# Turned weight blocks 14 to 17 placed behind the next period's scores, two late q units one or two loops later, half of w_out one loop earlier

## The chip, the core and the metric

The kernel runs on one core of a Trainium2 chip. That core has five engines with queues of their own, each served strictly in order: TensorE (PE: matmuls and transposes, results in PSUM), VectorE (DVE), ScalarE (ACT), GpSimd (POOL) and SyncE (SP, which here issues DMA only). The metric is device time in microseconds for one execution; the time of a kernel is the median of its runs.

## The reference, cut to what matters

Attention over 8 batches of 8 heads, 576 tokens and head size 64, in which each row keeps only the scores within `tau` of its maximum, and behind it a two-layer network on the 4608 tokens.

```python
scores = scale * np.matmul(q, k.transpose(0, 1, 3, 2))
thresh = np.max(scores, axis=-1, keepdims=True) - tau
scores = np.where(scores >= thresh, scores, -1000000000.0)
attn = np.exp(scores - np.max(scores, axis=-1, keepdims=True))
attn = attn / (np.sum(attn, axis=-1, keepdims=True) + 1e-09)
out = np.matmul(attn, v)
...
h = x @ w_in                      # 4608x512 by 512x2048
g = np.maximum(0.01 * h, h)
return (g @ w_out).astype(np.float32)
```

## The kernel before, in words

The attention is cut into *periods*. A period is one batch `b`, one quarter `m` of its first 512 query tokens (or the 64-token tail, `m == 4`) and two of the four pairs of heads; it has four score tiles of 128 queries by 576 keys. The order of all instructions is written out by hand: one `while` loop (L633) issues, in its turn `n`, the scores of period `n` (`st`), the turning of the weights of period `n-1` (`before`) and the value product of period `n-2` (`due`, since `PV_LAG` is 2). Each engine executes its own instructions in the order in which the loop issued them. In the text, "loop 3" is turn `n == 3`.

In one loop turn the work goes like this:

- `scores(st)` (L302) multiplies q by k on TensorE into the PSUM tile `sc`, in three products of fp16 halves (high by high, low by high, high by low). A marker instruction on another queue (`SIGNAL`, L279, POOL's or SP's) orders two pieces that share a bank. VectorE reads each tile out, negates it and takes the minimum (`copy_min`, L336).
- The first `plain` tiles get their weights from an exponential on ScalarE (`exp_plain`, L364) and a masking product on VectorE (`weights`, L376). The others get them from two ScalarE passes, a steep one and an exponential (`exp_steep`, L369: a "steep pair", lines 372 and 373). `plain` is 2 for the first two periods and 3 from then on.
- A period's weights, 18 blocks of 128 by 64 in pairs, must be turned. From period 3 on a DMA transpose issued by SP does it (`turn_w`, L387). For periods 0 to 2 (`here`) TensorE does it (`turn_w_here`, L393) and the result is copied from PSUM (`take_w`, L401): blocks 0 to 5 by way of an `h` bank, 6 to 13 and 14 to 17 by way of the one `o` bank. Blocks 14 to 17 are turned at the end of loop `n`, after the copy of blocks 6 to 13 by ScalarE, and ahead of `scores` of loop `n+1` (L752 to L760).
- `pv(due)` (L418) multiplies the turned weights by v, `evacuate` (L432) scales by the reciprocal row sums (`spread` turns these on TensorE, ScalarE copies them to `by`), and two periods make one group of 128 tokens for the network. `layer1` (L456, into `hp`, then ScalarE's leaky step to `g`) and `layer2` (L473, into `o`) are handed out over the loop turns, up to two of the first and four of the second in each.
- PSUM holds `sc` in five banks, two banks with the tag `h` (turned q and k, `by`, `pv`, `hp`, late units) and one with the tag `o`.
- q and k reach TensorE turned and split into two fp16 halves. For batch 0 units of the raw fp32 data are turned on TensorE (`turn32`, L196), and ScalarE writes the high half (`take_high`, L228), VectorE the low half (`take_low`, L234). Which unit is due in which loop stands in the tables `early32` and `late32` (L575 to L580). The unit `q32[s, 2]` covers token blocks 2 and 3 of head pairs `2s` and `2s+1`; period 4 is the first to need `q32[0, 2]`, and period 5 the first to need `q32[1, 2]`. From batch 1 on POOL splits the data ahead of the turning (`split_pool`).
- Loads: SP issues k, q and v, and the weight transposes stand on the same queue. `load_w` (L121) loads w_in (0 to 3) and w_out (4 to 7) in eight DMAs of 512 KB issued from POOL's queue, with a cast to fp16; `pool_at` names the loop turn.
- `idle(k, bank)` (L520) issues `2k` matmuls on blank data, whose result is not used. Loops 0 to 3 have some after the scores, and loop 3 twelve more (24 matmuls) ahead of its first `layer1`.

Of the kernel before, what the change touches and what calls it, by code (L numbers as in the profile page):

```python
# [33 lines left out]
def kernel(  # L34
# [86 lines left out]
    def load_w(i):  # L121
        if i < 4:
            return nc.gpsimd.dma_start(out=w_in16[:, :, ts(i, 512)],
                                in_=moe_w_in[:, ts(i, 512)].rearrange("(a p) f -> p a f", p=128))
        else:
            j = i - 4
            return nc.gpsimd.dma_start(out=w_out16[:, ds(4 * j, 4), :],
                                in_=moe_w_out[ds(512 * j, 512), :].rearrange("(j p) f -> p j f", p=128))
# [378 lines left out]
    def at(d, n, f):  # L507
        d.setdefault(n, []).append(f)
# [17 lines left out]
    def spare(tag):  # L526
        return ps.tile([128, 512], FP32, tag=tag, bufs=2 if tag == "h" else 1, name="spare")
# [47 lines left out]
    early32[0] = [k32[2], [q32[1, 0]]]  # L575
    late32[0] = k32[3]
    early32[1] = [[q32[0, 1]]]
    late32[1] = [q32[0, 2]]
    early32[2] = [[q32[1, 1]]]
    late32[3] = [q32[1, 2]]  # L580
    def load_w_in():

        loads = [load_w(i) for i in range(4)]
# [6 lines left out]
        at(pool_at, 1 + p // 2, lambda p=p: cast_v(0, p))  # L590
    at(pool_at, 1, lambda: cast_vtails(0))
    for i in range(4):
        at(pool_at, 1 if i < 2 else 4, lambda i=i: load_w(4 + i))

    def split_at(n, key):
        at(split_at_, n - 1, key)
# [35 lines left out]
    n = 0  # L632
    while n < N + PV_LAG or l1q or pending or l2q or stores:  # L633
        st = periods[n] if n < N else None
        before = periods[n - 1] if 1 <= n <= N else None
        due = periods[n - PV_LAG] if PV_LAG <= n < N + PV_LAG else None
        here = before and before.n < 3
        plain = 2 if n < 2 else 3
        keys, now32, late = turns_at.get(n, []), early32.get(n, []), late32.get(n)


        if n == 0:
            def between():
                copy_min(st, 0)
                copy_min(st, 1)
                take_low(k32[1])
                for x in now32:
                    turn32(x)
            scores(st, between)
            turn32(late)  # L650
        elif st:
            scores(st)
        bank = turn(keys) if keys else None
        for x in now32 if n else []:
            turn32(x)
        if here:
            before.wt = sb.tile([128, 2, 9, 128], FP16, tag="wT", bufs=4, name="wT")
            bank = ps.tile([128, 1024], FP16, tag="h", bufs=2, name="tp")
        if due:
            bank = spread(due, bank)  # L660
        if here:
            turn_w_here(before, 0, 6, bank[:, 0:768])
        for key in keys:
            take(key, 0, on_act)
        if due:
            take_spread(due, bank)
        for x in now32:
            take_high(x)
        if here:
            take_w(before, 0, 6, bank[:, 0:768], on_act)  # L670
        if st:
            copies(st, before, lambda: [take(key, 1, on_dve) for key in keys], now32)
            exp_plain(st, 0)
            if n == 0:
                exp_plain(st, 1)
                take_high(late)
                take_low(late)
        elif before:
            recip(before)
        work = [lambda key=key: split_pool(key) for key in split_at_.get(n, [])] + pool_at.get(n, [])  # L680
        for i, f in enumerate(work):
            mm = f()
            if i == 0 and before:
                behind_masks(mm, before)
        for key in keys:
            if key[1:] == ("t", "k"):
                widen_keys(key[0])
        if n >= 5:

            for f in small_at.get(n, []):  # L690
                f(small=nc.gpsimd)
        if n < 4:
            idle((4, 10, 8, 4)[n], spare("o"))
        if here:
            o = ps.tile([128, 1024], FP16, tag="o", bufs=1, name="wp")
            if n < 3:
                turn_w_here(before, 6, 8, o)
        elif before and st:
            turn_w(before)
        for f in loads_at.get(n, []) + (small_at.get(n, []) if n < 5 else []):  # L700
            f()
        while stores and (n >= N or n not in loads_at or len(stores) > 1):
            store()

        if due and (n == 3 or n > N):
            pv(due)
            if n > N:
                evacuate(due)
        if n == 3:
            turn_w_here(before, 6, 8, o)  # L710
            idle(12, spare("h"))
        for half in range(2):
            if half == 1 and n == 3:
                exp_steep(st, 3)
            for _ in range(2):
                if l2q:
                    layer2()
            if l1q:
                layer1()
            elif n >= N:  # L720
                settle()
            if half == 0:
                if st:
                    for i in range(1, plain if n else 0):
                        exp_plain(st, i)
                if here:
                    take_w(before, 6, 8, o, on_act)
                if late and n not in (0, 3):
                    turn32(late)
                    take_high(late)  # L730
                if n == N:

                    before.wt = sb.tile([128, 2, 9, 128], FP16, tag="wT", bufs=4, name="wT")
                    free = [(sc[:, ts(i, 512)].bitcast(FP16), 8 * i, m) for i, m in enumerate((8, 8, 2))]
                    for o, first, m in free:
                        turn_w_here(before, first, m, o)
                if due and n <= N:
                    if n != 3:
                        pv(due)
                    evacuate(due)  # L740
                if n == N:
                    a, *more = [take_w(before, first, m, o[:, 0 : 128 * m], on_dve if first else on_act)
                                for o, first, m in free]
                    for x in more:
                        tc.declare_no_dep(x.ins, a.ins, reason="other banks")
            elif st and n != 3:
                for i in range(plain, 4):
                    exp_steep(st, i)
        if n == 3:
            turn32(late)  # L750
            take_high(late)
        if here:  # L752
            o = ps.tile([128, 512], FP16, tag="o", bufs=1, name="wp")
            turn_w_here(before, 14, 4, o)
        for i in range(plain if st else 0):
            weights(st, i)
            if late and n and i == (2 if n == 3 else 0):
                take_low(late)
            if here and i == 1:
                take_w(before, 14, 4, o, on_dve)  # L760
        n += 1
# [1 line left out]
_INS = ['q', 'k', 'v', 'tau', 'moe_w_in', 'moe_w_out']  # L763
# [31 lines left out]
```

## Time and profile before

| | |
|---|---|
| median of 3 runs | 487.35 us (487.16 to 488.01) |
| the profiled execution | 485.95 us |
| its span, first to last instruction | 484.2 us |
| mean granted TensorE clock over the span | 0.996 |

Times in views of the profile are microseconds from the start of the span. A row of the timeline or of the chain gives the start, the length, the engine, the line of the kernel and the operation, as output `<-` inputs. Square brackets give the idle time of the engine just before, and what ended it. Groups give busy time and mean nanoseconds of one instruction. The "chain" is the work that ended last, followed back from the last instruction. A chain row's length is the time for which it held the chain; the same instruction's row in the timeline has its own length.

### The profile page before, as it was taken

To read this page: it belongs to the slowest core of one execution; us is meant where nothing else is said; L and a number is where in the kernel's file an instruction comes from. 1 tells how busy PE (TensorE), PEld (TensorE's weight loads), DVE (VectorE), ACT (ScalarE), POOL (GpSimd) and SP (SyncE) were. 2 spreads that over 40 slices of the span, in tenths; PEclk is the share of its full clock that TensorE was granted. 3 is DMA by queue.
4 is the path that set the end of the run, shared out by engine and by line. 5 is a ranking of instruction groups with operands and counts; after the bars stand their busy time and mean duration, and the time that the engine had idled before them with its cause. 6 is when DMAs were issued, how large, how long until landed. Compare 5 with 4: busy or idle time off the path is not lost.

```text
span 484.2 us, 25192 instructions
## 1 busy us (share of the span) xinstructions
PE 465.3 (96%) x10834; PEld 377.4 (78%) x10834; DVE 433.1 (89%) x1311; ACT 420.5 (87%) x781; POOL 215.0 (44%) x353
## 2 busy tenths in 40 slices
PE   7878799999999999999999999999999999999996
PEld 5667688888888888888888778888878788777774
DVE  3988789999999999999999989999999999999940
ACT  4898588999999999999999989999999899988862
POOL 2636545554465464454465574454456473000000
PEclk9999899999999999999999999999999999999999
DMA  9999987799899989789899988979899997655541
GB/s 176 233 218 189 205 189 165 153 187 199 181 177 189 237 168 173 156 164 212 178 189 192 185 188 185 151 180 192 185 184 203 193 184 123 123 122 123 123 95 45
DMA packets 206752, 83.68 MB, mean 173 GB/s; under 512 B 175792, under 2 KB 201392, under 8 KB 206640
## 3 DMA queue, kind: packets, MB, share of 16 engines
q1 hardware_dynamic: 199728, 74.79, 80.1%
q0 software_dynamic: 5504, 6.82, 7.4%
q8 instruction: 85, 1.39, 1.2%
q10 hardware_dynamic: 1408, 0.46, 0.4%
q14 instruction: 27, 0.22, 0.2%
HBM read 36.70 MB, written 9.44 MB: 95 GB/s over the span
## 4 chain that ended last, share of the span: by engine, by line
PE 87%; ACT 6%; DMA 4%; DVE 1%; issue 1%; SPq 0%; POOL 0%; POOLq 0%; ACTq 0%
PE hp L466 25%; PE o L479 25%; PE sc L297 21%; PE pv L426 8%; DMA wT<-w 4%; PE tp L410 3%; PE tp L186 3%; ACT w L373 1%; ACT e L367 1%; ACT s L372 1%; ACT wT L402 1%; PE sc L523 1%; DVE s L338 1%; ACT g L469 1%; ACT qT L232 0%
## 5 line engine op out<-in xcount | busy, mean ns | idle before, releaser
L338 DVE TENSOR_SCALAR_CACHE_REDUCE s<-sc 128x576 f32<-128x576 f32 x288 | 205.3, 753 | 17.4 <-PE sc L297 17.1
L466 PEld LDWEIGHTS <-win 128*64 128x64 f16 x4608 | 147.1, 110 | 28.8 <-DVE xt L437 1.1
L378 DVE SCALAR_TENSOR_TENSOR w<-s,th,e 128x576 f16<-128x576 f32 x214 | 164.4, 815 | 0.6 <-DVE x L445 0.2
L367 ACT ACTIVATE e<-s,mn 128x576 f16<-128x576 f32 x214 | 158.3, 778 | 0.0
L479 PE MATMUL o<-wout,g 128*64 128x512 f16 x1152 | 149.4, 381 | 0.4 <-DMA wout<-in_moe_w_out_dram 0.4
L466 PE MATMUL hp<-x,win 128*64 128x128 f16 x4096 | 137.1, 220 | 0.4 <-DVE kT L249 0.4
L469 ACT ACTIVATE g<-hp 128x512 f16<-128x512 f32 x144 | 86.1, 598 | 44.0 <-PE hp L466 43.9
L297 PE MATMUL sc<-kT,qT 64*128 64x384 f16 (+7 forms) x1920 | 120.5, 284 | 2.4 <-SPq L331 0.9
L297 PEld LDWEIGHTS <-qT 64*128 64x128 f16 (+1 forms) x1920 | 89.8, 97 | 19.7 <-SPq L331 2.0
L160 POOL TENSOR_SCALAR scaled<-raw 128x512 f32<-128x512 f32 x53 | 32.7, 616 | 148.2 <-DVE w L378 128.1
L479 PEld LDWEIGHTS <-g 128*64 128x64 f16 x1152 | 58.6, 110 | 29.6 <-issue 0.7
L171 POOL TENSOR_TENSOR half<-scaled,half 128x512 f16<-128x512 f32 (+1 forms) x68 | 71.7, 1054 | 5.8
L373 ACT ACTIVATE w<-s,minus_tau 128x576 f16<-128x576 f32 x74 | 57.4, 776 | 2.4
L372 ACT ACTIVATE s<-s,th 128x576 f32<-128x576 f32 x74 | 56.8, 767 | 0.7 <-DVE th L356 0.7
L426 PE MATMUL pv<-wT,v 128*64 128x128 f16 (+1 forms) x1600 | 53.0, 214 | 4.0 <-DMA wT<-w 2.8
L426 PEld LDWEIGHTS <-v 128*64 128x64 f16 x1600 | 45.8, 110 | 4.9 <-issue 4.0
L167 POOL CAST half<-scaled 128x512 f16<-128x512 f32 (+1 forms) x68 | 38.2, 562 | 4.4
L445 DVE TENSOR_TENSOR x<-pv,by 128x256 f16<-128x256 f32 x64 | 27.1, 424 | 8.1 <-PE pv L426 6.5
L416 ACT COPY by<-tp 128x256 f16<-128x256 f16 x72 | 26.8, 372 | 1.1 <-PE tp L397 1.1
L186 PEld LDWEIGHTS <-half 64*128 64x128 f16 x968 | 24.4, 95 | 3.5 <-DVE qT L239 1.4
L186 PE MATMUL tp<-ident,half 64*128 64x64 f16 x968 | 24.5, 190 | 1.0 <-DVE qT L239 1.0
L113 POOL CAST v<-vraw 128x256 f16<-128x256 f32 x64 | 24.0, 408 | 0.0
(61 smaller groups left out, 335.4 us busy)
## 6 DMA issues: line engine op xcount, KB each, us to landing
vraw<-in_v_dram SPq DMA_DIRECT2D x16, 512.0 KB, 5.4
out_dram<-osb SPq DMA_DIRECT2D x31, 256.0 KB, 4.0
raw<-in_q_dram SPq DMA_DIRECT2D x13, 512.0 KB, 4.9
raw<-in_k_dram SPq DMA_DIRECT2D x13, 512.0 KB, 5.1
win<-in_moe_w_in_dram POOLq DMA_DIRECT2D x4, 512.0 KB, 9.6
wout<-in_moe_w_out_dram POOLq DMA_DIRECT2D x4, 512.0 KB, 12.5
raw<-in_q_dram SPq DMA_DIRECT2D x12, 128.0 KB, 3.8
raw<-in_k_dram SPq DMA_DIRECT2D x10, 128.0 KB, 4.2
```

Source lines behind the costliest of these rows:

```text
L171: nc.gpsimd.tensor_tensor(out=halves[key][:, 1, 0:n, :, :], in0=scaled.pop(key)[:, 0:n, :, :], in1=halves[key][:, 0, 0:n, :, :], op=AX.sub ...
L186: nc.tensor.transpose(tps[key][r][:, x, t, :], half[rows, x, t, :, :].rearrange("p h d -> p (h d)"), ident[rows, rows])
L297: yield nc.tensor.matmul(out=o, lhsT=lhs, rhs=turned[st.b, "k"][rows, kx, pair, ds(key0, n)], start=(i == 0), stop=(i == 2), skip_group_ch ...
L338: return nc.vector.tensor_scalar(out=st.s[TILES[n]][:, :], in0=sc[:, ds(PLACE[TILES[n]], 576)], scalar1=-1.0 / UNIT, scalar2=None, op0=AX. ...
L367: nc.scalar.activation(out=st.e[t][:, :], in_=st.s[t][:, :], func=AF.Exp, bias=st.mn[:, n : n + 1], scale=-1.0)
L372: nc.scalar.activation(out=z, in_=z, func=AF.Prelu, bias=st.th[:, n : n + 1], scale=-1.0, alpha=1e20)
L373: nc.scalar.activation(out=w_of(st, t), in_=z, func=AF.Exp, bias=minus_tau[:, :], scale=1.0, accum_out=st.sum[:, c, h : h + 1])
L378: st.last = nc.vector.scalar_tensor_tensor(out=w_of(st, t), in0=st.s[t][:, :], scalar=st.th[:, n : n + 1], in1=st.e[t][:, :], op0=AX.is_le ...
L426: nc.tensor.matmul(out=st.pv[ds(64 * h, 64), c, ts(u, n)], lhsT=v16[st.b % 2][:, pair, blk, :], rhs=st.wt[:, c, blk - (blk > 4), ts(u, n)] ...
L466: nc.tensor.matmul(out=hp[ds(64 * c, 64), jj, :], lhsT=w_in16[:, i, ds(128 * (4 * u + jj) + 64 * c, 64)], rhs=g.x[:, i, :], start=(i == 0) ...
L469: nc.scalar.activation(out=g.g[:, ds(4 * u, 4), :], in_=hp[:, :, :], func=AF.Prelu, bias=0.0, scale=1.0, alpha=0.01)
L479: nc.tensor.matmul(out=g.o[ds(64 * c, 64), :], lhsT=g.g[:, j, ds(64 * c, 64)], rhs=w_out16[:, j, :], start=(j == 0), stop=(j == 15), skip_ ...
```

## The change

```diff
     early32[1] = [[q32[0, 1]]]
-    late32[1] = [q32[0, 2]]
+    late32[3] = [q32[0, 2]]
     early32[2] = [[q32[1, 1]]]
-    late32[3] = [q32[1, 2]]
+    late32[4] = [q32[1, 2]]
...
     for i in range(4):
-        at(pool_at, 1 if i < 2 else 4, lambda i=i: load_w(4 + i))
+        at(pool_at, 1 if i < 2 else 3, lambda i=i: load_w(4 + i))
...
         here = before and before.n < 3
-        plain = 2 if n < 2 else 3
+        rest = due and due.n < 3
+        plain = 2 if n < 2 or n == 4 else 3
...
         elif st:
             scores(st)
+        if rest:
+            o = ps.tile([128, 512], FP16, tag="o", bufs=1, name="wp")
+            turn_w_here(due, 14, 4, o)
         bank = turn(keys) if keys else None
...
         if st:
-            copies(st, before, lambda: [take(key, 1, on_dve) for key in keys], now32)
+            def taken():
+                for key in keys:
+                    take(key, 1, on_dve)
+                if rest:
+                    take_w(due, 14, 4, o, on_dve)
+            copies(st, before, taken, now32)
...
         if n == 3:
+            turn32(late)
             turn_w_here(before, 6, 8, o)
-            idle(12, spare("h"))
...
                         exp_plain(st, i)
+                if n == 3:
+                    take_high(late)
                 if here:
                     take_w(before, 6, 8, o, on_act)
...
-        if n == 3:
-            turn32(late)
-            take_high(late)
-        if here:
-            o = ps.tile([128, 512], FP16, tag="o", bufs=1, name="wp")
-            turn_w_here(before, 14, 4, o)
+        if n == 4:
+            take_low(late)
         for i in range(plain if st else 0):
             weights(st, i)
-            if late and n and i == (2 if n == 3 else 0):
+            if late and (n == 3 and i == 1 or n > 4 and i == 0):
                 take_low(late)
-            if here and i == 1:
-                take_w(before, 14, 4, o, on_dve)
         n += 1
```

It has five parts.

1. Blocks 14 to 17 of periods 0, 1 and 2 are turned at the start of the next loop turn, behind its scores (loops 2, 3 and 4), and VectorE copies them between the first and the second tile that it reads from the new scores.
2. The unit `q32[0, 2]` moves from loop 1 to loop 3 and `q32[1, 2]` from loop 3 to loop 4. In loop 3 the unit is turned ahead of blocks 6 to 13, its high half is written ahead of ScalarE's copy of these blocks, and its low half after VectorE's second weights. In loop 4 the low half is written ahead of the weights.
3. In loop 4 `plain` is 2: the third tile of period 4 gets its weights from a steep pair on ScalarE, and VectorE's product for it goes.
4. The last two of the four w_out loads are issued in loop 3, behind the splitting of the first k unit of batch 1, and no longer in loop 4.
5. The 24 matmuls on blank data in loop 3 go.

## The prediction

> **What bounds the kernel now.** I read the page first, then the granted clock and the DMA rate over stretches, then the chain of waits from the start to 120 us.
>
> ```profile
> PE 465.3 (96%) x10834; PEld 377.4 (78%) x10834; DVE 433.1 (89%) x1311; ACT 420.5 (87%) x781; POOL 215.0 (44%) x353
> ...
> L367 ACT ACTIVATE e<-s,mn 128x576 f16<-128x576 f32 x214 | 158.3, 778 | 0.0
> ...
> L373 ACT ACTIVATE w<-s,minus_tau 128x576 f16<-128x576 f32 x74 | 57.4, 776 | 2.4
> L372 ACT ACTIVATE s<-s,th 128x576 f32<-128x576 f32 x74 | 56.8, 767 | 0.7 <-DVE th L356 0.7
> ```
>
> TensorE is busy for 465.3 of 484.2 us, so only some 19 us are open, and the diff touches periods 1 to 4 alone. Every later period does the same work in the same order, so the question is how much earlier the kernel falls into step. Columns of the next rows: stretch, length, busy time of PE, PEld, DVE, ACT, POOL, then granted clock, DMA share, GB/s.
>
> ```profile
> 28.00:36.00 8.00, 7.57 (x169) 6.72 (x170) 6.66 (x22) 6.86 (x12) 2.38 (x3) 1.00 1.22 212
> 36.00:44.00 8.00, 6.60 (x154) 5.53 (x152) 7.19 (x22) 6.15 (x12) 3.89 (x5) 1.00 0.94 158
> 44.00:52.00 8.00, 7.78 (x181) 6.44 (x178) 7.47 (x24) 6.92 (x15) 4.42 (x7) 1.00 1.27 245
> 54.20:56.60 2.40, 0.02 (x1) 0.00 (x1) 1.00 (x4) 1.94 (x4) 2.40 (x6) 1.00 0.63 134
> 57.20:60.70 3.50, 3.50 (x49) 2.61 (x45) 2.64 (x7) 0.00 (x0) 0.47 (x1) 0.52 1.24 210
> ```
>
> From 54.20 to 56.60 TensorE does almost nothing, and right behind that, from 57.20 to 60.70, its clock is granted at 0.52. The chain of waits (start, length, what) names the cause:
>
> ```profile
> 44.95 11.54 DMA wT<-w
> ...
> 56.63 0.75 PE pv L426 x20
> 57.38 1.65 PE o L479 x8
> 59.02 1.71 PE hp L466 x32
> ```
>
> The weights of period 4 are turned by a DMA transpose issued at 44.95, which lands at 56.49; period 6's value product `pv` has to wait for it. The earlier part of the chain is a hand-over between ScalarE (ACT) and TensorE:
>
> ```profile
> 20.62 0.50 ACT qT L232
> ...
> 31.03 0.37 ACT by L416
> ...
> 37.06 0.50 ACT qT L232
> ...
> 39.33 1.08 PE hp L466 x32
> 40.42 0.56 PE pv L426 x20
> 40.98 0.86 PE o L479 x8
> 41.84 0.89 PE hp L466 x32
> 42.73 1.57 PE sc L297 x16
> ```
>
> One row of the timeline belongs between the first two:
>
> ```profile
> 28.43 0.41 PE L397 MATMUL wp<-ident,w 128*64 128x128 f16 x8 [2.35 <-ACT wT L402]
> ```
>
> At 28.43 the last four blocks of period 2's weights (`wp`, blocks 14 to 17 of 18) are turned as soon as ACT has copied blocks 6 to 13 out of the one `o` bank, and only behind them come the scores of period 3 and what ACT needs to go on at 31.03.
>
> **The change part by part. First: the four blocks go behind the scores.** The same 8 transposes (0.41 us on the path at 28.43) and the same copy by VectorE (DVE) remain, one loop turn later. What goes is the order "ACT copy, `wp`, scores, ACT". Between 28.43 and 31.03 lie 2.60 us, in which ACT has one steep pair to do, 0.767 + 0.776 = 1.54 us by the groups. So ACT idles for about 1.06 us there, and that is what the edit can return; the scores of period 3 then start when DVE has read the previous ones. The `o` bank still has one buffer, so `wp` now waits for it behind the scores. Queued behind that wait are the transposes for `by`, the idle matmuls and `pv`, and they need ACT's same copy or the one just before it anyway, so I cost the moved wait at nothing; without that cover it would cost the 0.41.
>
> **Second: the two late q units.** The first, two head pairs by two token blocks, leaves loop 1 for loop 3, which takes ACT's 0.50 at 20.62 off the path. The second leaves loop 3 for loop 4. In loop 3 there is thus one unit before and one after; it only stands earlier there, ahead of the weight copy. Together with the 1.06 ACT should reach the end of period 3 at 37.56 - 0.50 - 1.06 = 36.0. Before, the key transposes of period 4 also waited for the low half of that unit on DVE, and `hp` started at 39.33, 1.77 behind ACT's copy. Now they wait only for ACT's last `g`. If the whole 1.77 stays, `hp` starts at 37.8; if DVE's part of it (a third to a half) falls away, at 37.0. That is a lead of 1.5 to 2.3 us.
>
> Loop 4 gets the second unit, and its price stands here:
>
> ```profile
> 34.56 0.66 PE L211 MATMUL tp<-ident,raw 128*128 128x128 f32 x4
> ...
> 44.83 0.57 ACT L249 COPY qT<-tp 128x512 f16<-128x512 f16 x1
> ...
> 47.22 0.75 PE L426 MATMUL pv<-wT,v 128*64 128x128 f16 x20
> ```
>
> Four fp32 transposes cost 0.66 us of TensorE, ahead of `pv`, and since they take one of two `h` banks, `pv` now waits for ACT to empty `hp`: 0 to 0.6, I take 0.3. The scores of period 5 then start at 42.73 - 1.9 + 0.66 + 0.3 = 41.8, or 41.1 at the good end.
>
> **Third: `plain` is 2 in loop 4.** The third tile goes from a plain exponential on ACT (0.778) and a mask on DVE to a steep pair on ACT (1.54). This pair stands behind the second `hp`, where ACT had 42.73 to 44.83, 2.1 us, to its next copy. From 41.1 to 41.8 it is now 2.1 + 1.54, so that copy comes at 44.7 to 45.4 instead of 44.83. The lead is mostly spent on ACT. After it come on ACT `by`, a first exponential and `g`, whose `hp` is ready sooner than before, and then `pv`, until now at 47.22; there I take 0.4 us of lead as left (**term 1**). Bounds: the plain sum of ACT's changes in period 4 if none of the head start arrives, 0.50 + 1.54 - 0.78 = 1.26 against the 0.50 saved in loop 1, a loss of about 0.8, I keep -0.9; and the whole lead of TensorE at the good end, 42.73 - 41.1 = +1.6. My 0.4 lies nearer to the ACT side because the row at 44.83 sets what follows.
>
> **Fourth: w_out's second half one loop earlier.** The queue of SyncE (SP), which issues the transposes, and the landing of the w_out loads:
>
> ```profile
> 36.84 2.94 SPq L389 DMA_TRANSPOSE wT<-w  x1
> 39.88 0.51 SPq L75 DMA_DIRECT2D raw<-in_k_dram  x1
> 40.49 0.55 SPq L99 DMA_DIRECT2D vraw<-in_v_dram  x1
> 41.14 2.20 SPq L106 DMA_DIRECT2D vrawt<-in_v_dram  x2
> 44.95 7.92 SPq L389 DMA_TRANSPOSE wT<-w  x1
> ```
> ```profile
> wout<-in_moe_w_out_dram POOLq DMA_DIRECT2D x2, 512.0 KB, 10.2
> ```
>
> The last row is for the two loads issued from GpSimd's (POOL's) queue in loop 4. Issuing one transpose takes SP 2.94 us, and 7.92 when loads are backed up ahead of it. The 11.54 us are thus 7.92 of issue and 3.62 behind it. Ahead of it stand 1.15 MB from SP and 1.05 MB of w_out on POOL's queue. The DMA engines moved 158 GB/s from 36 to 44 us and 245 from 44 to 52. They can hold (245 - 158) x 8 us = 0.70 MB more in the first stretch. If w_out is in flight there already, SP's own 1.15 MB, issued from 39 to 43 us, drain alone at 245 GB/s in 4.7 us, by about 47 to 48. The transpose issued at 44.7 to 45.4 then has its issue over at 47.7 to 48.5 and lands at 51.3 to 52.1. TensorE wanted it at 54.2 (the start of the idle stretch) less term 1, near 53.8, so the wait of 54.2 to 56.63 goes: 2.4 us (**term 2**, bounds 0 and 2.4). On POOL the two issues move past the splitting of period 4's second unit, which is only done earlier; and they move ahead of the marker that releases the second half of period 4's scores, which at POOL's 44% busy hides them.
>
> With the wait goes the slow clock: `o` and `hp` at 57.38 and 59.02 took 1.65 + 1.71, against 0.86 + 0.89 at 40.98 and 41.84, so 1.61 us (**term 3**, bounds 0 and 1.61). Late next would be period 5's transpose; it stands behind the same SP queue, which moves up by some 4 us with it.
>
> **The idle matmuls** (24 in loop 3) lay in TensorE's slack while ACT was the chain; I cost their loss at nothing, and what it would cost without that cover is the clock case below. Trainium skill, "TensorE: Matmul & The Clock Gate", Part 4: PE-mode transpose, says that transposes do not count as TensorE activity for the clock as other matmuls do. Loop 3 loses real matmuls and gains transposes, so the page speaks against this edit; by it the sum would be that of the clock case. No stretch of this trace is made of transposes alone for long enough to settle it.
>
> **Sum.** 0.4 + 2.4 + 1.6 = 4.4 us. The profiled execution took 485.95 (its span of 484.2 and 1.75 around it), so 481.55; the runs' median lies 1.4 higher at 487.35, so 482.95, rounded to **483.0**.
>
> **The rivals.**
> *ACT eats more than the lead* (term 1 at -0.9, terms 2 and 3 as above): a gain of 3.1, **484.2**. For it: the row at 44.83. Against it: ACT is busy for only 6.15 of 8 us from 36 to 44.
> *The clock falls in loop 3.* After the idle 2.4 us at 54.20 it fell to 0.52; in loop 3 there would be mostly transposes for some 4 us. One `hp` and one block of scores, 1.08 + 1.57 us, would double, and about 1 us of that lies in slack: 1.6 lost, **484.6**. Against it: ahead of 28.43 TensorE idles for 2.35 us, and the clock of the stretch behind it (28 to 36 us) reads 1.00.
> *The load's move does not do what it is for*: the first w_out half is still moving when the second is issued, the same bytes pass, and the transpose lands at 56.49 as now. Then the wait swallows the lead: **487.35**. For it: the DMA share of 0.94 from 36 to 44. Against it: only 158 GB/s there.
> *The jam moves to period 3's transpose* (the slower side). This one is issued near 36.1, now right among the w_out loads. If it too takes 7.92 us, SP is free at 44.0 rather than 39.8, its three loads (3.46 us) end at 47.5, and period 4's transpose starts there. With 7.92 once more it lands at 47.5 + 7.92 + 3.62 = 59.0, 2.5 later than now: **489.8**. It decides the sign from the point where that landing passes 56.49, that is when both issues together are stretched by over 7.4 us. For it: w_out shares the engines with whatever is issued beside it. Against it: w_out is then the only load ahead, on another queue, and SP's has room.
>
> **How the numbers follow.** Forecast 0.60, ACT 0.12, clock 0.08, no change 0.08, jam 0.12. Two runs that differ by under 0.2% (1 us) can't be told apart. Faster: 0.60 + 0.12 + 0.08 = 0.80; within 0.2%: 0.08; slower: 0.12. The low end is 487.35 - (1.6 + 2.4 + 1.6) = 481.75, less 0.25 for the spread of the runs, 481.5. The high end takes in both faster rivals and a wait that goes only in part, 487.0; left out are the last two rivals.
>
> **What would show it.** Right: no TensorE wait on `wT` near 54 us, a granted clock of 1.00 from 52 to 62, the issue of period 4's transpose near 3 us instead of 7.92, the scores of period 3 before 28, `pv` of loop 5 at 46.5 to 47.4, and a steady state that begins 4 to 5 us earlier. The step on ACT is wrong if `pv` of loop 5 comes after 47.5 or before 46; the step on the loads if a transpose is issued for over 5 us between 35 and 50; and the prediction as a whole if `pv` still waits for `wT` in loop 5 or 6.

## The result and the profile after

| | before | changed |
|---|---|---|
| median of the runs | 487.16 us (486.45 to 488.01, 7 runs) | 484.70 us (482.95 to 486.71, 7 runs) |
| ratio, 95% interval | | 0.9949 [0.9925, 0.9972] |
| profiled execution, its span | 485.95, 484.2 us | 483.62, 481.9 us |
| mean granted clock of that execution | 0.996 | 1.000 |

Of all the runs in this document one, the 489.31 us among e9's four, is in a slower state, and the median and ratio of e9 below are of the other three.

The changed kernel is 2.5 us faster, inside the range that was forecast and 1.7 us above the forecast of 483.0. But the wait that the forecast made its gain from is still there. First the parts of TensorE's timeline of the changed kernel that mark its path: the scores (`sc`) of periods 3, 5, 7 and 9, the first `hp` of loop 4, and `pv` of loops 5, 6 and 7.

```profile
26.03 1.64 PE L297 MATMUL sc<-kT,qT 64*128 64x384 f16 x24
...
37.22 1.08 PE L466 MATMUL hp<-x,win 128*64 128x128 f16 x32 [0.29 <-DVE kT L249]
...
41.49 1.65 PE L297 MATMUL sc<-kT,qT 64*128 64x384 f16 x24
...
47.39 0.75 PE L426 MATMUL pv<-wT,v 128*64 128x128 f16 x20 [0.61 <-DMA wT<-w]
...
56.15 0.75 PE L426 MATMUL pv<-wT,v 128*64 128x128 f16 x20 [2.31 <-DMA wT<-w]
...
58.59 1.64 PE L297 MATMUL sc<-kT,qT 64*128 64x384 f16 x24
...
63.82 0.75 PE L426 MATMUL pv<-wT,v 128*64 128x128 f16 x20 [0.79 <-DMA wT<-w]
...
73.42 1.77 PE L297 MATMUL sc<-kT,qT 64*128 64x384 f16 x24
```

The same view of the kernel before, for the rows that the prediction did not show: the scores of period 3 and 7, `pv` of loop 7, the scores of period 9.

```profile
28.78 1.64 PE L297 MATMUL sc<-kT,qT 64*128 64x384 f16 x24
...
60.66 1.65 PE L297 MATMUL sc<-kT,qT 64*128 64x384 f16 x24
...
65.23 0.75 PE L426 MATMUL pv<-wT,v 128*64 128x128 f16 x20
...
74.81 1.77 PE L297 MATMUL sc<-kT,qT 64*128 64x384 f16 x24
```

TensorE does get ahead: 2.75 us at the scores of period 3, 2.1 us at `hp` (39.33 before), 1.2 at the scores of period 5 (42.66). ScalarE takes the lead back, as worked out. Then `pv` of loop 6, at 56.63 before, starts at 56.15, still behind 2.31 us of waiting for period 4's transposed weights. The queue of SP in the changed kernel shows why.

```profile
35.73 8.10 SPq L389 DMA_TRANSPOSE wT<-w  x1
43.94 0.51 SPq L75 DMA_DIRECT2D raw<-in_k_dram  x1
44.54 1.11 SPq L99 DMA_DIRECT2D vraw<-in_v_dram  x1
45.75 1.28 SPq L106 DMA_DIRECT2D vrawt<-in_v_dram  x2
47.13 5.24 SPq L389 DMA_TRANSPOSE wT<-w  x1
```

Period 3's transpose took 8.10 us to issue, where it took 2.94, so SP's loads went out 4 us later and period 4's transpose at 47.13 instead of 44.95. Its issue was shorter, and its data were there at 56.0, within half a microsecond of before (56.5). The stretches of the changed kernel (columns as in the prediction):

```profile
28.00:36.00 8.00, 6.06 (x130) 4.92 (x131) 7.43 (x24) 7.93 (x15) 4.59 (x7) 1.00 1.23 207
36.00:44.00 8.00, 7.56 (x175) 6.33 (x176) 7.14 (x22) 5.73 (x12) 3.07 (x5) 1.00 1.29 181
44.00:52.00 8.00, 6.62 (x156) 5.46 (x152) 6.35 (x17) 7.04 (x14) 2.90 (x5) 1.00 1.28 225
52.00:57.00 5.00, 2.69 (x66) 1.96 (x62) 3.39 (x12) 4.20 (x10) 4.85 (x9) 1.00 0.91 203
57.00:62.00 5.00, 5.00 (x114) 4.09 (x112) 4.69 (x13) 3.27 (x7) 2.98 (x5) 1.00 0.98 172
```

From 28 to 52 us the DMA engines moved 8 x (207 + 181 + 225) = 4.90 MB, and 8 x (212 + 158 + 245) = 4.92 MB before. What came earlier into one stretch left the next.

What did change is the clock. The stretch behind the wait in the kernel before, in the same view:

```profile
57.00:62.00 5.00, 5.00 (x77) 3.99 (x73) 2.64 (x7) 1.23 (x2) 1.29 (x3) 0.66 1.18 211
```

Granted 0.66 over these 5 us before, 1.00 after, with the wait only 0.1 us shorter. From `pv` of loop 6 to the scores of period 7 it is 60.66 - 56.63 = 4.03 us before and 58.59 - 56.15 = 2.44 after: 1.59 us. With 0.48 from the landing, less 0.66 by which the next interval, up to `pv` of loop 7, grew (a new wait of 0.79 there), that is the 1.4 us by which the scores of period 9 come earlier. The other 0.9 us of the two spans arises later, and the first experiment shows what that is worth.

### The profile page after: what moved, and what is told of

Read it like the earlier page. It is cut to its first block, busy times and chain, and to the rows that moved or that the text cites. A ratio compares the mean times of both kernels' runs of the same rounds, so it can differ in the third digit from the quotient of the medians.

```text
span 481.9 us, 25139 instructions
## 1 busy us (share of the span) xinstructions
PE 463.4 (96%) x10810; PEld 375.5 (78%) x10810; DVE 432.0 (90%) x1309; ACT 421.3 (87%) x783; POOL 215.5 (45%) x353
## 4 chain that ended last, share of the span: by engine, by line
PE 86%; ACT 5%; DMA 4%; DVE 3%; issue 1%; SPq 1%; POOL 0%; POOLq 0%; ACTq 0%
PE hp L466 25%; PE o L479 25%; PE sc L297 21%; PE pv L426 8%; DMA wT<-w 4%; PE tp L410 3%; PE tp L186 3%; DVE s L338 1%; ACT w L373 1%; ACT s L372 1%; ACT e L367 1%; PE sc L523 1%; DVE w L378 1%; ACT wT L402 0%; ACT g L469 0%
## 5 line engine op out<-in xcount | busy, mean ns | idle before, releaser
L372 ACT ACTIVATE s<-s,th 128x576 f32<-128x576 f32 x75 | 57.6, 768 | 0.7 <-DVE th L356 0.7
L338 DVE DVE_READ_ACCUMULATOR s<-sc 128x1 f32 x288 | 24.1, 84 | 0.0
```

The lines of the kernel that those rows point to most:

```text
L338: return nc.vector.tensor_scalar(out=st.s[TILES[n]][:, :], in0=sc[:, ds(PLACE[TILES[n]], 576)], scalar1=-1.0 / UNIT, scalar2=None, op0=AX. ...
L372: nc.scalar.activation(out=z, in_=z, func=AF.Prelu, bias=st.th[:, n : n + 1], scale=-1.0, alpha=1e20)
```

## The experiments

Each row below is one kernel. "Issue 3" and "issue 4" are the times for which SP issued the transposes of periods 3 and 4, "wait" is that of `pv` in loop 6 for `wT`, "landing 4" the start of period 4's issue plus its time to landing, "clock" the granted clock from 57 to 62 us, "period 9" the start of its scores, all in one profiled execution. Ratios are to the kernel before, run on the same chip in the same session, and only they compare kernels across sessions: its median was 488.55 us beside e0, e1, e2 and e5, 488.25 beside e4, e6, e7 and e8, and 488.08 beside e3, e9, e10 and e11. Three profiles run late from the start: their scores of period 3 begin 1.4 (e4), 1.1 (e9) and 1.4 us (e11) after those of the kernel that they were made from, ahead of anything that the edits touch. The account from the two traces was that the jam had moved to period 3's transpose and that only the clock had changed behind it; the rivals to it stand in the expectations.

| kernel | median us (runs) | ratio [95%] | issue 3, 4 | landing 4 | wait | clock | period 9 | span |
|---|---|---|---|---|---|---|---|---|
| before | 487.16 (7) | | 2.94, 7.92 | 56.5 | 2.41 | 0.66 | 74.81 | 484.2 |
| changed | 484.70 (7) | 0.9949 [0.9925, 0.9972] | 8.10, 5.24 | 56.0 | 2.31 | 1.00 | 73.42 | 481.9 |
| e0 changed, again | 485.53 (12) | 0.9944 [0.9915, 0.9973] | 8.14, 4.05 | 56.5 | 2.18 | 0.67 | 74.84 | 485.5 |
| e1 w_out back in loop 4 | 485.43 (12) | 0.9942 [0.9914, 0.9970] | 4.08, 7.42 | 56.6 | 2.85 | 0.66 | 75.10 | 482.9 |
| e2 before, w_out moved | 485.44 (12) | 0.9931 [0.9905, 0.9958] | 7.54, 3.97 | 55.3 | 1.87 | 1.00 | 72.91 | 481.9 |
| e5 before, blocks moved | 486.42 (12) | 0.9963 [0.9935, 0.9990] | 3.83, 7.44 | 56.4 | 3.75 | 0.69 | 75.11 | 483.8 |
| e6 half of w_out not loaded | 481.67 (4) | 0.9878 [0.9846, 0.9910] | 4.06, 3.17 | 50.0 | none | 1.00 | 70.32 | 480.2 |
| e7 half of k, q, v of batch 1 later | 486.15 (10) | 0.9964 [0.9939, 0.9988] | 8.53, 4.74 | 53.0 | none | 1.00 | 76.34 | 485.3 |
| e8 e7, w_out in loop 4 | 484.13 (8) | 0.9931 [0.9909, 0.9952] | 3.69, 3.73 | 52.5 | none | 1.00 | 72.33 | 481.8 |
| e4 `plain` 3 in loop 4 | 487.73 (1) | | 8.05, 5.25 | 57.9 | 2.30 | 0.67 | 76.15 | 486.0 |
| e9 half of v of batch 1 later | 483.20 (3) | 0.9884 [0.9821, 0.9946] | 8.23, 5.38 | 53.9 | none | 1.00 | 73.46 | 483.1 |
| e10 e9, w_out in loop 4 | 484.74 (10) | 0.9945 [0.9914, 0.9976] | 4.46, 5.79 | 54.8 | none | 1.00 | 73.50 | 484.7 |
| e11 before, v later | 486.04 (10) | 0.9970 [0.9937, 1.0004] | 2.99, 6.98 | 57.7 | 0.99 | 1.00 | 75.09 | 485.9 |
| e3 blank matmuls back | 486.00 (10) | 0.9955 [0.9931, 0.9978] | 8.74, 5.36 | 57.6 | 2.18 | 0.70 | 75.87 | 486.5 |

**e0: the changed kernel once more.**

> The changed kernel once more, to see how much its trace varies. Theory J (the jam moved: beside the second half of w_out, period 3's transpose is slow to issue, and the queue of SP passes the delay on): the issue of period 3's transpose takes 6 to 9 us again, pv of loop 5 or of loop 6 waits for wT for 1 to 4 us in all, and the time lies between 483 and 487 us as the wait moves from one loop to the other and the clock falls or not. Rival F (my forecast; the first trace was an unlucky one): the issue takes about 3 us, no wait for wT before 60 us, 482 to 483.5.

The ratio repeats. The profile doesn't: here are TensorE's rows from `pv` of loop 6 to the scores of period 9, and the stretch behind the wait.

```profile
56.60 1.05 PE L426 MATMUL pv<-wT,v 128*64 128x128 f16 x20 [2.18 <-DMA wT<-w]
...
60.70 1.64 PE L297 MATMUL sc<-kT,qT 64*128 64x384 f16 x24
...
74.84 1.77 PE L297 MATMUL sc<-kT,qT 64*128 64x384 f16 x24
```
```profile
57.00:62.00 5.00, 5.00 (x75) 4.04 (x72) 2.64 (x7) 1.20 (x2) 2.04 (x4) 0.67 0.93 188
```

The same kernel, a wait 0.13 us shorter, and the clock fell. At period 9 this execution is where the kernel before was, to 0.03 us. So the 1.59 us of clock is not a fixed gain: it is there in some executions. Behind period 9, span less start is 408.5 us in the first profile of this kernel and 410.7 in the second (409.4 before; 407.8 to 411.2 in all fourteen). The 0.9 us above is therefore within what one kernel shows by itself, and a span of one profile can't rank these kernels; the runs must.

**e1 and e2: the load's move taken out, and the load's move alone.** e1 is the changed kernel with

```diff
-        at(pool_at, 1 if i < 2 else 3, lambda i=i: load_w(4 + i))
+        at(pool_at, 1 if i < 2 else 4, lambda i=i: load_w(4 + i))
```

and e2 the kernel before with the opposite edit of the same line.

> The changed kernel with the second half of w_out issued in loop 4, as before the change. J: the issue of period 3's transpose falls from 8.1 to about 3 us, pv of loop 5 does not wait; period 4's transpose is slow again (issue 7 to 8 us, landing near 56), pv of loop 6 waits 2 to 4 us and the clock falls behind it: 485 to 487.5. Rival P (the transpose is slow because it is issued 1.1 us earlier, into the first half of w_out): the issue stays near 8 us and the time near 484.7. Rival N (the place of these loads does not matter): as the changed kernel in both.

> The kernel before with only the second half of w_out moved to loop 3. J: period 3's transpose, issued near 36.8, takes 6 to 9 us to issue, and lands near 47.5 to 48.5; pv of loop 5, wanted at 47.2, waits 0 to 1.3; period 4's lands near 55 to 57: no gain that can be measured, 486 to 488. Rival L (moving the load is what gains, by taking it away from period 4's transpose): the wait at loop 6 falls from 2.4 to under 1 us and the clock stays at 1.00: 483 to 485.

SP's two transposes and `pv` of loop 6, first in e1:

```profile
35.88 4.08 SPq L389 DMA_TRANSPOSE wT<-w  x1
...
45.50 7.42 SPq L389 DMA_TRANSPOSE wT<-w  x1
```
```profile
56.73 0.75 PE L426 MATMUL pv<-wT,v 128*64 128x128 f16 x20 [2.85 <-DMA wT<-w]
```

and in e2:

```profile
36.75 7.54 SPq L389 DMA_TRANSPOSE wT<-w  x1
...
47.70 3.97 SPq L389 DMA_TRANSPOSE wT<-w  x1
```
```profile
55.45 0.75 PE L426 MATMUL pv<-wT,v 128*64 128x128 f16 x20 [1.87 <-DMA wT<-w]
```

The place of the load decides which of the two issues is long, and with either the landing is at 55.3 to 56.6. So e1's rows are those of J. In e2 J's rows came (issue 7.54, landing 55.3), but its forecast of no gain that can be measured failed; L's clock of 1.00 came, and its wait of under 1 us did not (1.87). Each half of the change alone gains as much as the whole: three intervals around 0.994 that overlap almost fully. That the gains don't add up fits one limit in common; it does not show which.

**e5: only the first part, in the kernel before** (blocks 14 to 17 behind the scores, nothing else).

> The kernel before with only blocks 14 to 17 moved behind the next scores; late units, plain, idle matmuls and w_out as before. By my steps: ACT's idle time of 1.06 us ahead of 31.03 goes, period 4 begins about 1 us earlier, but period 4's transpose still lands near 56 and its wait swallows that: 487 within 1 us, with a wait for wT in loop 6 of 3 us or more. Rival (the lead is kept to the end): 486 or less.

Scores of period 3, then `pv` of loops 5 and 6:

```profile
26.54 1.64 PE L297 MATMUL sc<-kT,qT 64*128 64x384 f16 x24
...
46.38 0.75 PE L426 MATMUL pv<-wT,v 128*64 128x128 f16 x20
...
56.59 1.21 PE L426 MATMUL pv<-wT,v 128*64 128x128 f16 x20 [3.75 <-DMA wT<-w]
```

The part gives TensorE 47.22 - 46.38 = 0.84 us, near the 1.06 that was read from ScalarE's idle time. All of it goes into the wait, which is 1.34 us longer, and `pv` of loop 6 starts where it did, as expected. In the runs it still gains 0.0037, barely apart from nothing.

By now the theory was that the start of the kernel is bound by what the DMA engines have to move: period 4's transpose lands when the work ahead of it is through, in whatever order it stands. Against it stood the theory that only the order on SP's queue counts.

**e6: less to move.** The changed kernel without the DMAs of w_out's second half; GpSimd copies the first half into its place in loop 4, so the second layer computes with other weights.

```diff
+    for i in range(2):
+        at(pool_at, 1, lambda i=i: load_w(4 + i))
     for i in range(4):
-        at(pool_at, 1 if i < 2 else 3, lambda i=i: load_w(4 + i))
+        at(pool_at, 4, lambda i=i: nc.gpsimd.tensor_copy(out=w_out16[:, ds(8 + 2 * i, 2), :], in_=w_out16[:, ds(2 * i, 2), :]))
```

> The changed kernel without the DMA of the second half of w_out: POOL copies the first half into its place in loop 4, so the second layer computes with other weights. Theory V (volume: period 4's transpose landed at 55.5 to 56.7 in all six traces, whatever the place of w_out and the lead of TensorE, because the DMA engines are full from the start to that point): 1.05 MB less at 245 GB/s is 4.3 us, so it lands near 52, pv of loop 6 does not wait, the clock stays at 1.00, period 3's transpose issues in about 4 us; steady state 3 to 4 us earlier, 480.5 to 483. Rival Q (only the order on the queue of SP matters, k and v of batch 1 ahead of the transpose): it lands at 54 or later and pv of loop 6 still waits 1 us or more: 484 to 486.

Period 4's transpose on SP; then `pv` of loop 6 and the scores of period 9:

```profile
45.32 3.17 SPq L389 DMA_TRANSPOSE wT<-w  x1
```
```profile
53.52 0.72 PE L426 MATMUL pv<-wT,v 128*64 128x128 f16 x20
...
70.32 1.77 PE L297 MATMUL sc<-kT,qT 64*128 64x384 f16 x24
```

No wait, no slow clock, and period 9 starts 4.5 us earlier than before, near the forecast's sum of 4.4, in a kernel that leaves out two DMAs. The runs gain 0.0122 of 488.25, 6.0 us; where the other 1.5 arises was not followed. SP's order is that of the changed kernel, so the theory that only this order counts is out. The volume theory had the rows right, except that the data land at 50.0, 2 us ahead of its forecast. But e6 takes away two things at once, the megabyte to be moved and the loads of GpSimd's queue that run beside the transposes, and does not tell one from the other.

**e4, e7, e8: other ways to make room.** e4 puts `plain` back to 3 in loop 4. e7 loads the second half of batch 1's k and the first half of its v in loop 5 instead of 4, and the second half of its q in loop 6 instead of 5; e8 also has w_out back in loop 4.

```diff
-        plain = 2 if n < 2 or n == 4 else 3
+        plain = 2 if n < 2 else 3
```
```diff
-            rows, t_at, v_at, casts = (0, 2, 4, 5), (3, 6), (4, 7, 4), (6, 7, 9, 10, 9)
+            rows, t_at, v_at, casts = (0, 2, 5, 6), (3, 6), (5, 7, 5), (6, 7, 9, 10, 9)
```

> The changed kernel with plain 3 in loop 4, as before the change: one plain exponential and one mask in place of a steep pair. By my step ACT's first copy of loop 5 comes 0.8 us earlier (near 44.4 instead of 45.23). V: pv of loop 5 still waits until wT lands near 47.4, and loop 6 until 56: no gain. Rival (ACT sets loop 5): pv of loop 5 starts before 46.8.

> The changed kernel with k and v of batch 1 (1.15 MB, first read in loop 6) loaded in loop 5, behind period 4's transpose, and the q parts of loop 5 in loop 6. V: the same bytes are ahead only of what can wait, so period 4's transpose issues in about 3 us near 45 and lands by 52; period 3's is still slow beside w_out (issue 6 to 8 us, pv of loop 5 waits 0 to 1). pv of loop 6 does not wait, no slow clock: 481 to 483. Rival (the wait only moves again, to POOL's splitting of the late k or to period 5's transpose): a wait of 2 us or more for wT or for half in loops 6 to 8, 484 to 486.

> As the one before, but the second half of w_out back in loop 4. V: now nothing stands beside period 3's transpose (issue 3 to 4 us, no wait in loop 5) and only w_out beside period 4's (issue 3 to 6 us, landing 51 to 54): 481 to 483, the same as with loop 3 or better by up to 1 us. Rival: w_out beside period 4's transpose stretches its issue to 7 us again, landing near 56, 484 to 486.

e4 is one run, 1.4 us late from the scores of period 4 on (34.86 against 33.42) for reasons ahead of the edit; it waits 1.31 and 2.30 us for `wT` in loops 5 and 6, as V had it, so it shows no gain of its own. In e7 period 4's transpose is issued at 45.33 and lands at 53.0, early enough, but now it stands right behind period 3's. That one lands at 50.1, against 47.3 in the changed kernel, though no load of k or v was issued between them. `pv` of loop 5 shows it (the clock behind it reads 0.83 from 52 to 57 us):

```profile
50.18 1.23 PE L426 MATMUL pv<-wT,v 128*64 128x128 f16 x20 [3.42 <-DMA wT<-w]
```

So V's 481 to 483 us failed in e7 (486.15), and the rival missed where the wait would go. In e8 V has its rows: issues of 3.69 and 3.73 us, period 4's data at 52.5, no wait for `wT` at all. Its time failed all the same (484.13): e8 waits 1.0 us for GpSimd's marker in the scores of period 7, and 4 us of its chain are the late loads of q. Its ratio of 0.9931 can't be told from that of the changed kernel.

**e9, e10, e11: only v of batch 1 later.** Its first half and its tails, 0.64 MB, leave loop 4 for loop 6, in the changed kernel (e9), with w_out in loop 4 besides (e10), and in the kernel before (e11).

```diff
-            rows, t_at, v_at, casts = (0, 2, 4, 5), (3, 6), (4, 7, 4), (6, 7, 9, 10, 9)
+            rows, t_at, v_at, casts = (0, 2, 4, 5), (3, 6), (6, 7, 6), (8, 8, 9, 10, 9)
```

> The changed kernel, with only the v of batch 1 (0.64 MB in four loads on SP's queue) moved from loop 4 to loop 6 and its casts one or two loops later. V (the bytes ahead of period 4's transpose set its landing, whatever their order): at the 160 to 210 GB/s of the trace 0.64 MB are 3 to 4 us, so that transpose lands near 52.5 to 53.5 and pv of loop 6 (near 53.6 when nothing holds it) waits for under 0.5; scores of period 7 at 56 to 57; ratio to before 0.988 to 0.991. W (the wait only moves): pv of loop 5 or of loop 7 waits for wT for 1 us or more instead, or a later transpose does, and the ratio stays at 0.993 to 0.996 as in the two runs with k, q and v deferred.

> The run with v of batch 1 in loop 6, and w_out's second half back in loop 4 besides. V: the bytes ahead of period 4's transpose are the same, it lands within 0.7 us of that run, and the ratio is within 0.002 of it; period 3's transpose has its issue over in 4 us again. If the place of w_out decides after all: period 4's issue is stretched to 7 us, it lands near 56 and pv of loop 6 waits for 2 us or more.

> The kernel before, with only the v of batch 1 moved from loop 4 to loop 6. V: the wait of 2.4 us and the slow clock behind it go without any part of the change: pv of loop 6 near 54.2, scores of period 7 at 57.5 to 58, ratio 0.990 to 0.993; against the changed kernel with the same edit it is 0.5 to 1.5 us slower, which is what the lead of TensorE is worth once nothing swallows it. Rival (the lead is worth nothing, ScalarE has spent it): the two are equal within 0.5 us.

`pv` of loops 6 and 7, in e9 and then in e10:

```profile
55.44 0.72 PE L426 MATMUL pv<-wT,v 128*64 128x128 f16 x20
...
63.87 0.75 PE L426 MATMUL pv<-wT,v 128*64 128x128 f16 x20 [1.33 <-DMA wT<-w]
```
```profile
54.90 0.75 PE L426 MATMUL pv<-wT,v 128*64 128x128 f16 x20 [1.16 <-ACT g L469]
...
63.90 0.75 PE L426 MATMUL pv<-wT,v 128*64 128x128 f16 x20 [2.11 <-DMA wT<-w]
```

The wait for period 4's transpose goes in both, and comes back one loop later for period 5's; in e9 `pv` of loop 5 waits besides, 1.27 us for period 3's. `pv` of loop 7 starts at 63.82 in the changed kernel, 63.87 in e9 and 63.90 in e10; that e9, which starts 1.1 us late, agrees with the others to 0.1 is partly chance. On V's account the ratio should have been 0.988 to 0.991 in both and the landings within 0.7 us. The ratio fell in e10 (0.9945), and e9's interval with three runs is too wide to say more. The landings are 54.8 in e10 and, less the late start, 52.7 in e9: the place of w_out counts too. W had the main point: the wait only moves.

In e11 it is the volume theory that fails. With 0.64 MB less ahead of it, period 4's transpose lands at 57.7, or 56.3 less the late start, against 56.5 in the kernel before. The wait is shorter only because TensorE comes later, by the late start and by a wait for w_out:

```profile
50.98 1.05 PE L479 MATMUL o<-wout,g 128*64 128x512 f16 x8 [1.61 <-DMA wout<-in_moe_w_out_dram]
...
57.83 0.75 PE L426 MATMUL pv<-wT,v 128*64 128x128 f16 x20 [0.99 <-DMA wT<-w]
```

With w_out in loop 4 of the kernel before its second half can land too late for `layer2`. e11's ratio can't be told from 1, and 0.990 to 0.993, as V had it, lies outside its interval; neither of its two expectations on the lead is settled. From 44 to 52 us SP's queue moved 0.65 MB in e11 where it had moved 1.12, and GpSimd's 0.94 where it had moved 0.82. So the bytes ahead of a transpose do not set its landing alone. These rows point to what GpSimd's queue has under way at the time; how much each counts stays open.

**e3: the 24 blank matmuls back.**

```diff
             turn_w_here(before, 6, 8, o)
+            idle(12, spare("h"))
```

> The changed kernel with the 24 matmuls on blank data put back in loop 3. My step: they lay in slack, and the granted clock of 28 to 44 us reads 1.00 with and without them, so the ratio to before is that of the changed kernel (0.993 to 0.997) and pv of loop 6 waits for wT for 1.9 to 2.4 us as there. Rival (TensorE has no slack left in loop 3 once the blocks have moved): the first hp of loop 3 starts 0.7 us or more later than in the changed kernel (37.22), and the kernel is 0.3 to 0.7 us slower.

The first `hp` of loop 4, and period 3's transpose on SP:

```profile
37.79 1.08 PE L466 MATMUL hp<-x,win 128*64 128x128 f16 x32 [0.29 <-DVE kT L249]
```
```profile
35.69 8.74 SPq L389 DMA_TRANSPOSE wT<-w  x1
```

They cost TensorE 37.79 - 37.22 = 0.57 us there, so they did not lie wholly in slack once the blocks had moved. (The row at 37.22 is loop 4's; the first `hp` of loop 3, right behind the blank matmuls, goes from 32.41 to 33.93.) `pv` of loop 5 then starts at 49.06, 1.67 us later than in the changed kernel, behind a wait of 1.72 for `wT`: there the transpose sets the time and not the 0.57. The ratio of 0.9955 overlaps that of the changed kernel, and the wait of 2.18 in loop 6 is the one that was expected.

## Why the prediction came out as it did

**Time and mechanism part ways.** Term 1 has its size at `pv` of loop 6, by another cause, and is swallowed. Term 2 did not come (0.1 of 2.4, and 0.48 at the landing). Term 3 came whole in one profiled execution of the changed kernel and not in the other. That 484.70 lies near the forecast of 483.0 is luck: the chain of reasons did not hold. By its own test, that `pv` does not wait for `wT` in loop 5 or 6, the prediction as a whole is wrong.

**First and second part: right.** Scores of period 3 before 28: 26.03. `hp` at 37.0 to 37.8: 37.22. Scores of period 5 at 41.1 to 41.8: 41.49. The blocks alone gave 0.84 of the 1.06 us (e5).

**Third part: the right number by another cause.** ScalarE's copy was to come at 44.7 to 45.4 and its row is

```profile
45.23 0.56 ACT L249 COPY qT<-tp 128x512 f16<-128x512 f16 x1
```

The lead was put at 0.4 us at `pv` of loop 5, and so at `pv` of loop 6 (53.8 in place of 54.2). At loop 6 the number fits: less its wait `pv` would have started at 56.15 - 2.31 = 53.84. At loop 5 it doesn't. In e6, where nothing waits for `wT`, `pv` of loop 5 starts at 47.25, held by ScalarE, where it was 47.22 before:

```profile
47.25 0.75 PE L426 MATMUL pv<-wT,v 128*64 128x128 f16 x20 [0.50 <-ACT g L469]
```

So ScalarE eats the lead whole (the rival *ACT eats more than the lead*, with -0.9, went too far). What is left at loop 6 comes from w_out: in the kernel before, its second half lands late for `layer2` there,

```profile
52.27 1.05 PE L479 MATMUL o<-wout,g 128*64 128x512 f16 x8 [0.39 <-DMA wout<-in_moe_w_out_dram]
```

and `pv` of loop 6 was wanted 54.22 - 49.66 = 4.56 us behind the scores of period 6. In the changed kernel, where that wait is gone, it is 53.84 - 49.83 = 4.01. e2, with none of the first three parts, has 55.45 - 1.87 = 53.58, more lead than the whole change. The prediction did not count this wait, and the two errors cancel.

**Fourth part: the step that failed** is "They can hold (245 - 158) x 8 us = 0.70 MB more in the first stretch", and with it "its issue over at 47.7 to 48.5 and lands at 51.3 to 52.1". With it goes a cost that the sum left out: period 3's transpose, which stands beside the moved loads, was left at an issue of 2.94 us. It took 8.10, SP's loads went out from 43.94 and not from 39.88, and period 4's data landed at 56.0. The DMA view from 36 to 44 us, by queue (packets, MB, share of the 16 engines' time), shows the two queues against each other; q0 has what GpSimd issues, w_out above all, and q1 what SP issues. First before, then changed:

```profile
q1 hardware_dynamic: 2486, 0.74, 46.6%
q0 software_dynamic: 503, 0.50, 46.2%
```
```profile
q0 software_dynamic: 1280, 1.27, 104.9%
q1 hardware_dynamic: 619, 0.16, 22.4%
```

w_out's half came into the stretch, and SP's queue, with period 3's transpose at its head, fell from 0.74 MB to 0.16. In all the stretch moved 181 GB/s, 0.18 MB more, while the share rose from 0.94 to 1.29 (over 1, so the times of the packets overlap). The 245 GB/s that the room was counted by is no rate of the w_out loads: in their 104.9% of 8 us they moved 1.27 MB, which is 151 GB/s for a full share, while SP's queue had 0.74 MB in 46.6%, 198 GB/s. e2 alone shows the same (1.29 MB at 98.3% and 0.16 MB at 26.2%), so the move of the load does it and no other part of the change. The Trainium skill, "DMA: Bandwidth & Descriptors", section "Latency and other measured facts", gives 261 GB/s for one kernel's DMA transposes with a non-contiguous middle dimension and about 350 to 400 for contiguous ones; here the stretches with transposes and loads together moved 158 to 245, and no run here has the transposes by themselves.

**The rivals.** *The jam moves to period 3's transpose* had the places right: SP free at 44.0 (43.94), period 4's transpose from 47.5 (47.13). Its price was wrong, since it put the second issue at 7.92 us again; that came out at 5.24 (4.05 in e0). Together the two issues were stretched by 8.10 + 5.24 - 2 x 2.94 = 7.46 us, and this rival had put at 7.4 the point where the landing is as before. *The load's move does not do what it is for* had that landing right, "the transpose lands at 56.49 as now" (56.0), given a chance of 0.08. Its time of 487.35 was wrong: it held the slow clock for fixed, and did not see the wait for w_out that the move takes away.

**Fifth part and the clock.** No clock fell in loop 3: 28 to 44 us read 1.00 without the blank matmuls. The rule of the Trainium skill quoted in the prediction would have made it 484.6 by a slow stretch there; no profile has one. The price of the blank matmuls, taken as nothing, was 0.57 us of lead, covered by the wait.

**What the gain is.** In e0's session the mean granted clock over the span is 0.9939 in 35 runs of the kernel before and 0.9964 in 12 of the changed one. 0.0025 x 485 us = 1.2 us; one slow stretch of 3.5 us at 0.52 takes 0.48 x 3.5 / 485 = 0.0035 from the mean. So, as an estimate, somewhat under half of the 2.7 us between the two (0.0056 x 488.5) goes with fewer slow stretches. Where the rest arises is open: e0's own profile shows nothing of it by period 9, and behind that the executions scatter by more.

## What to carry to other kernels

Before counting on room in the DMA engines, take the rate of the queue that is to fill it, and look at what stands beside it: here a rate read from one mix of transfers was not that of another, and what went into the stretch drove the transpose out. When a reordering moves a stall from one transfer to the next and the landing stays put, ask what all the orders have in common. Here only leaving out a load (e6) took the stall away without another in its place; moving loads on met the next wait (e8, e9, e10). A number that fits is no proof of its cause: check it at a second place, and in a kernel that has only one part of the change. Where a wait is about as long as those behind which the clock falls, compare many executions, since one profile with the slow stretch and one without differ by more than the change.

## What the hardware showed besides

The time for which SP holds one DMA transpose ranges from 2.94 to 8.74 us for the same shape at nearly the same place (periods 3 and 4). It goes with what another queue has under way: period 3's takes 7.5 to 8.7 us in the seven kernels with w_out's second half in loop 3, and 2.9 to 4.5 in the other seven (e6 has no second half).

The granted clock fell behind waits of 2.18 (e0, e3), 2.30 (e4), 2.41 (before) and more, and did not behind waits of 1.87 (e2), 2.11 (e10) and 2.31 us (the changed kernel). Near 2.3 us both happen, so the length of the gap alone does not decide. The traces' records of the granted clock show what does. In each of the seven profiles with a slow stretch between 50 and 63 us it lasts 3.41 us at 0.50, and it begins a whole number of 3.41 us (13 to 16) after the record of full clock begins, which is at 4.28 to 10.89 us of the span. The fall at the end of the kernel lies on the same grid in all fourteen (138 to 141). Here is TensorE's busy time (the first figure behind the comma) in the cells of that grid around the wait, in the kernel before and in the first profile of the changed one; the granted clock is third from the end.

```profile
53.90:57.31 3.41, 1.00 (x34) 0.87 (x30) 1.30 (x4) 2.24 (x4) 3.41 (x8) 1.00 0.73 153
57.31:60.73 3.42, 3.42 (x45) 2.53 (x41) 2.64 (x7) 0.00 (x0) 0.36 (x1) 0.50 1.25 210
```
```profile
51.80:55.21 3.41, 2.04 (x46) 1.35 (x44) 3.41 (x12) 3.41 (x9) 3.26 (x6) 1.00 0.98 220
55.21:58.63 3.42, 2.48 (x62) 2.12 (x64) 1.80 (x5) 0.99 (x2) 2.65 (x5) 1.00 0.91 190
```

Before, the whole wait lies in one cell, and the next cell runs at half clock. In the changed kernel's first profile a boundary at 55.21 cuts the wait in two, and no cell is idle enough; in e0's the wait lies whole in the cell from 53.48 to 56.90 (1.24 us busy) and the clock falls. From 20 to 480 us of all fourteen profiles, each cell in which TensorE was busy for at most 1.33 us (there are seven) is followed by a slow one, and no cell with 1.47 or more is. (At the very start of e11, from 4.28 us, one cell with 2.04 is.) So whether this wait is punished depends on where the grid lies in that execution, and that one execution of the changed kernel kept its clock was chance. The Trainium skill, "TensorE: Matmul & The Clock Gate", Part 1, "What's actually happening", describes a free-running activity window of about 3.4 us and a clock that is either half or full. The traces agree with both: 3.41 us, and 0.50 or 1.00. Its section "Why this matters for your kernels" allows gaps up to about 3 us; here the clock fell behind 2.18, and the measurement decides.
